# Threshold attention and a gated MLP in one kernel: score matmuls in quadrants with their tail first, and the transposes of q and k as second job

## The chip, the core and the metric

The kernel runs on one core of a Trainium2 chip. The metric is device time in microseconds (us) from one execution of the whole program. Engines are named as in the profile: PE is the matmul engine and PEld its weight loads, DVE the vector engine, ACT the scalar engine, POOL the GpSimd engine, SP the engine whose queue issues most of the DMAs. `L575` means line 575 of the kernel before.

## The reference, cut to what matters

Eight batches, eight heads, 576 rows, head size 64. An attention in which only scores close to their row's maximum survive, then a gated MLP with a mix over the rows:

```
scores = 0.125 * q @ k.T                        # per head, 576 x 576
thresh = max(scores, axis=-1) - tau             # tau = 0.02
scores = where(scores >= thresh, scores, -1e9)
attn   = softmax(scores) @ v
x      = attn with the heads side by side       # 8 x 576 x 512
h      = relu(x @ w_in)                         # 512 -> 1024
u, v   = h[..., :512], h[..., 512:]
v_n    = (v - mean(v)) / sqrt(var(v) + 1e-6)
v_s    = w_spatial @ v_n + b_spatial[:, None]   # 576 x 576 over the rows
out    = (u * v_s) @ w_out                      # float32, 8 x 576 x 512
```

The scores are computed from float32 operands: with a threshold of 0.02 below the maximum, a score decides whether a row of v counts at all. The other products take bf16.

## The kernel before, in words

**Pairs and steps.** Heads are worked on two at a time, 32 pairs `i` in all. Head 0 of a pair lies on partitions 0 to 63, head 1 on 64 to 127. The 576 query rows of a pair are four chunks of 128 rows, `c` = 0 to 3, and 64 rows that remain. The remainders of an even and the next odd pair are put together into one more chunk, `c` = 4. A step is one (i, c): even pairs have the steps 0, 1, 2, 3 and odd pairs 4, 0, 1, 2, 3, which makes 144 steps, numbered from 0 (lines 766 to 768).

**A score** (`scores`, L563). A step writes one tile `s` of three PSUM banks from a pool of two tiles, so the score of step g+2 needs what ACT reads of step g's tile to be finished. For a main chunk there are, for each head, one float32 matmul of 64 x 128 weights against keys 0 to 511 (L575): the two heads take the upper and lower 64 rows of the array. Then the tail, one matmul of 128 x 128 (L578), gives keys 512 to 575 of both heads: its moving operand `kd` is block-diagonal, with the last 64 keys of head 0 in one corner and those of head 1 in the other, copied there by POOL (L269). In a `c` = 4 step there are two pairs, so each matmul has 64 columns of weights and one of two halves of the PSUM partitions. The profile shows a float32 matmul as two passes, so a main score has four rows of L575 and two of L578, and a `c` = 4 score eight and four.

**Behind a score.** DVE takes the negated maximum of each row (L616); ACT makes the exponentials `e` (L639, or L633 and L635 in steps in which ACT also does the threshold); DVE, where ACT has not done it, applies the threshold (L597); a DMA transposes the result into `pT`.

**The jobs of a step.** `step` (L604) first issues the score, then a list `fs` of further jobs. A job is a triple: the engine that takes its result out of PSUM ("act" or "dve"), its matmuls `mm`, and the evacuation `ev`. The first two jobs of the list are issued right behind the score, and those that ACT evacuates have their `ev` there, ahead of the step's exponentials on ACT. Later jobs have their matmuls issued at the end of the step. All results share the pool `ps_f` of two banks (`bank`, L221), handed out in turn: the third job of a step takes the bank of the first one and so waits for its `ev`.

The jobs that matter here:
- `qk_main(i, which)` (L238): four float32 transposes of q or k of the next pair (L246), evacuated by ACT (L251, L253). In steps c = 0 (q) and c = 2 (k).
- `qk_rem(i)` (L256): one transpose with the last 64 rows of q and of k (L261), evacuated by ACT (L264); then POOL makes `kd` (L269). In steps c = 1.
- `pv` (L309) and `pv_rest` (L336): attention times v, 18 bf16 matmuls of 65 or 130 columns (L290, L295), evacuated by DVE (L302, L304).
- `moe_v`, `moe_u`, `moe_s`, `moe_o` (L427 to L557): the MLP of a batch, four or five bf16 matmuls of 512 columns each (L436, L478, L508, L537); the last `u` and `s` are 16 and 20 matmuls of 64 columns (L483, L513), and the last `v` has 64 columns of weights (L421, L424). All are evacuated by ACT but `moe_s`, by DVE.
- `x_pe`, `pr_pe`, `ws_pe` (L360 to L411): bf16 transposes in the first third of the run, evacuated by ACT.

**The order.** The MLP of batch b begins at step 26 + 18 b, one job a step in the order of the string `ORDER` (L781), so the work repeats every 18 steps. The list of a step is put together in lines 838 to 850 with the transposes of the next pair at the head, then the `pv` jobs, then the MLP's. Line 851 sorts it: jobs for ACT ahead of jobs for DVE, `pv_rest` last; the sort keeps the order among equals.

Of the kernel before, what the change touches and what calls it, by code (L numbers as in the profile page):

```python
# [17 lines left out]
def kernel(  # L18
# [17 lines left out]
    nc = tc.nc  # L36
# [6 lines left out]
    P = 128  # L43
# [35 lines left out]
    def clear():  # L79
        nc.vector.memset(kd_ring[0], 0.0)  # L80
        nc.gpsimd.memset(ld_ring[0][2][64:128, :, 4, :], 0.0)
        for t in vx_ring:
            nc.gpsimd.memset(t[0:64], 0.0)
        nc.gpsimd.memset(kd_ring[1], 0.0)
        nc.gpsimd.memset(ld_ring[1][2][64:128, :, 4, :], 0.0)
        for t in v_ring:
            nc.vector.memset(t[:, :, D:D + 1], 1.0)
            nc.vector.memset(t[64:128, 4, D:D + 1], 0.0)
            nc.vector.memset(t[0:64, 5, D:D + 1], 0.0)
            nc.vector.memset(t[64:128, 10, D:D + 1], 0.0)  # L90
        for t in vn_ring:
            nc.vector.memset(t[64:128, 4, :], 1.0)
# [9 lines left out]
    def load(i, n, w, eng=nc.sync):  # L102

        b, hp = divmod(i, HP)
        t = ld_ring[i // 2 % 2][w][:, 2 * (i % 2):2 * (i % 2) + 2 * n]
        src = (q, k, v)[w][b, 2 * hp:2 * hp + 2 * n]

        def main():
            eng.dma_start(
                out=t[:, :, 0:4, :],  # L110
                in_=src[:, 0:512, :].rearrange("h (p c) d -> p h (c d)", c=4))

        def rest():

            u = ld_ring[i // 2 % 2][(0, 0, 2)[w]][(slice(0, 64), slice(64, 128), slice(0, 64))[w]]
            eng.dma_start(out=u[:, 2 * (i % 2):2 * (i % 2) + 2 * n, 4, :],
                          in_=src[:, 512:576, :].rearrange("h p d -> p h d"))

        def rest_b():
            nc.sync.dma_start(  # L120
                out=vx_ring[i // 2 % 2][64:128],
                in_=src.rearrange("(j h) s d -> h s j d", h=2)[1, 512:576])
        return [main, rest] + ([rest_b] if w == 2 else [])

    def view(t, off, dims):

        return bass.AP(t.tensor, t.offset + off, [t.ap[0]] + dims)
# [93 lines left out]
    def bank(dtype=F32, n=512):  # L221
        if wide:

            turn[0] += 1
            if turn[0] % 8 not in (2, 3):
                return wide[0].tile([P, n], dtype, name="t")
        return ps_f.tile([P, n], dtype, name="f")
# [5 lines left out]
    qks, pts, xns, xts = {}, {}, {}, {}  # L233
# [4 lines left out]
    def qk_main(i, which):  # L238
        hold = {}

        def mm():
            if which == 0:
                qks[i] = qkT.tile([P, 2, S], F32, name="qkT")
            t = hold["t"] = bank()
            for c in range(4):
                nc.tensor.transpose(out=t[:, c * P:(c + 1) * P], in_=nat[i][which][:, c, :],  # L246
                                    identity=identf)

        def ev():
            if which == 0:  # L250
                nc.scalar.mul(out=qks[i][:, 0, 0:512], in_=hold["t"], mul=scale)  # L251
            else:
                nc.scalar.copy(out=qks[i][:, 1, 0:512], in_=hold["t"])  # L253
        return "act", mm, ev

    def qk_rem(i):  # L256
        hold = {}

        def mm():
            t = hold["t"] = bank()  # L260
            nc.tensor.transpose(out=t[:, 0:P], in_=nat[i][0][:, 4, :], identity=identf)  # L261

        def ev():
            nc.scalar.copy(out=qks[i][:, :, 512:576],  # L264
                           in_=hold["t"][:, 0:P].rearrange("p (w s) -> p w s", w=2))
            kd = kd_ring[i % 2]
            for lo in (0, 64):
                hs = slice(lo, lo + 64)
                nc.gpsimd.tensor_copy(out=kd[hs, hs], in_=qks[i][hs, 1, 512:576])  # L269
        return "act", mm, ev  # L270
# [292 lines left out]
    def scores(i, c):  # L563

        s = ps_s.tile([P, 1536], F32, name="s")
        if c < 4:
            who = [(i, slice(c * P, (c + 1) * P), slice(0, P))]
        else:  # L570
            who = [(i - 1 + k, slice(512, 576), slice(64 * k, 64 * k + 64)) for k in range(2)]
        for h in range(2):
            hs = slice(64 * h, 64 * h + 64)
            for n, m, rows in who:
                nc.tensor.matmul(out=s[rows, 1024 * h:1024 * h + 512], lhsT=qks[n][hs, 0, m],  # L575
                                 rhs=qks[n][hs, 1, 0:512], start=True, stop=True)
        for n, m, rows in who:
            nc.tensor.matmul(out=view(s[rows], 512, [[448, 2], [1, 64]]), lhsT=qks[n][:, 0, m],  # L578
                             rhs=kd_ring[n % 2], start=True, stop=True)
        return view(s, 0, [[960, 2], [1, S]])  # L580

    def on_act(i, c):
# [21 lines left out]
    def step(i, c, fs):  # L604

        s = scores(i, c)
        while held:
            held.pop(0)()
# [174 lines left out]
    for b in range(B):  # L783
        n = dict.fromkeys("vuso", 0)
        for j, t in enumerate(ORDER):
            f = {"v": moe_v, "u": moe_u, "s": moe_s, "o": moe_o}[t]
# [17 lines left out]
    with tc.manual_schedule():  # L804
        for w in (0, 1):
            for f in load(0, 1, w, (nc.sync, nc.scalar)[w]):
                f()
        make_identity(nc, identf)
        clear()
        nc.vector.memset(ntau, -float(tau))  # L810
        nc.vector.memset(mhalf, -0.5)
        nc.scalar.activation(out=ctau, in_=ntau, func=ACT.Exp)
        nc.vector.tensor_copy(out=identb, in_=identf)
        for w in (0, 1):
            for f in load(1, 1, w):
                f()
        for f in load(0, 2, 2):
            f()
        for j in range(3):
            load_w_in(j)  # L820
        for _ in range(14):
            nc.tensor.transpose(out=ps_f.tile([P, 512], F32, name="f")[:, 0:P], in_=identf,
                                identity=identf)
        shape_first()
        first()
        shape_qk(1)
        queue = []
        for g, (i, c) in enumerate(steps):
            if c == 2 and i + 2 < NPAIR:
                shape_qk(i + 2)  # L830
            if c == 0:
                shape_v(i)
            if c == 0 and i % 2 and i + 3 < NPAIR or g == 0:
                for w in range(3):
                    queue.extend(load(i + (3 if g else 2), 2, w))
            if g in chores:
                chores[g][0](chores[g][1])
            fs, small_ones = [], []
            if i + 1 < NPAIR and c < 3:
                fs.append(qk_rem(i + 1) if c == 1 else qk_main(i + 1, c // 2))  # L840
            if i and c == (2 if i % 2 else 3):
                fs.append(pv(i - 1, 0))
            if i > 1 and c == 4:
                fs.append(pv(i - 2, 1))
            if i % 2 and c == 3:
                fs.append(pv(i - 1, 1))
            if i % 2 and i > 1 and c == 1:
                small_ones = [pv_rest(i // 2 - 1)]
                fs += small_ones
            fs += [f(*a) for f, *a in jobs.get(g, [])]  # L850
            fs.sort(key=lambda f: (f[0] == "dve", f in small_ones))
            sends += queue[:1 if g > 3 else 2]
            del queue[:1 if g > 3 else 2]
            step(i, c, fs)

        def run(*fs):
            for f in fs:
                f[1]()
                f[2]()
                for f in sends:  # L860
                    f()
                sends.clear()
        while held:
            held.pop(0)()
        mask()
        inner.close()
        wide.append(ctx.enter_context(tc.tile_pool(name="ps_t", bufs=6, space=PSUM,
                                                  reuse_waits="tile")))
        for _, f in later:
            f()  # L870
        last = [f(b, j) for f, b, j in last]
        run(last[0], pv_rest(NPAIR // 2 - 1), *last[1:3], x_pe(NPAIR - 2), *last[3:6],
            pv(NPAIR - 1, 0), *last[6:], pv(NPAIR - 1, 1), moe_s(Z - 1, 0), moe_s(Z - 1, 1),
            x_pe(NPAIR - 1, True), *[moe_s(Z - 1, j) for j in range(2, 5)])
        rest = last_gmlp(Z)
        next(rest)
        run(moe_u(Z, 0), moe_u(Z, 1))
        next(rest)
        run(*[moe_u(Z, j) for j in range(2, 5)], *[moe_o(Z - 1, j) for j in range(4)])
        next(rest)  # L880
        next(rest, None)
# [35 lines left out]
```

## Time and profile before

| what | value |
|---|---|
| median of 5 runs | 480.62 us |
| lowest and highest | 479.24 and 485.34 us |
| the profiled execution | 479.62 us |
| its span, first to last instruction | 477.8 us |
| around the span | 1.8 us |
| granted PE clock, mean | 1.00 |
| first and last matmul of a score (L575 and L578) | 8.0 and 434.3 us |
| PE, DVE, ACT busy from 120 to 180 us | 57.75, 53.14, 52.26 us of 60 |
| POOL busy from 120 to 180 us | 30.73 us of 60 |

The profile is of one execution. Its page gives busy times, then the span in 40 slices with the busy share of each in tenths. A timeline has one row per group of instructions that follow each other on an engine: start, length, engine, line, operation, output and inputs, tile of the array (rows * columns), operand shape, count. A wait row names who waited, for whom, the total in us, how often, and the longest. Matmuls are pipelined, so a row's length includes the time until the last result is out; what an operation costs PE is read from the distance between starts.

### The profile page before, as it was taken

To read this page: it belongs to the slowest core of one execution; us is meant where nothing else is said; L and a number is where in the kernel's file an instruction comes from. 1 tells how busy PE (TensorE), PEld (TensorE's weight loads), DVE (VectorE), ACT (ScalarE), POOL (GpSimd) and SP (SyncE) were. 2 spreads that over 40 slices of the span, in tenths; PEclk is the share of its full clock that TensorE was granted. 3 is DMA by queue.
4 is the path that set the end of the run, shared out by engine and by line. 5 is a ranking of instruction groups with operands and counts; after the bars stand their busy time and mean duration, and the time that the engine had idled before them with its cause. 6 is when DMAs were issued, how large, how long until landed. Compare 5 with 4: busy or idle time off the path is not lost.

```text
span 477.8 us, 9901 instructions
## 1 busy us (share of the span) xinstructions
PE 448.0 (94%) x3691; PEld 237.0 (50%) x3691; DVE 409.7 (86%) x563; ACT 390.3 (82%) x677; POOL 226.6 (47%) x403
## 2 busy tenths in 40 slices
PE   7678888889999999999999999999999999999995
PEld 4344545444545545454554545455554545445542
DVE  4989898989889997999889888899889998898573
ACT  4799899999879797888979898788978888797251
POOL 3553344895437543574417652475336743252021
PEclk9999999999999999999999999999999999999999
DMA  7979899969888999888889999987997989677523
GB/s 230 251 167 210 190 234 205 199 149 206 168 194 197 171 208 228 214 164 180 200 165 237 182 215 181 214 174 179 187 214 209 182 182 199 149 113 111 150 88 111
DMA packets 226127, 88.48 MB, mean 185 GB/s; under 512 B 196896, under 2 KB 221600, under 8 KB 226080
## 3 DMA queue, kind: packets, MB, share of 16 engines
q1 hardware_dynamic: 225424, 86.98, 85.7%
q8 instruction: 29, 0.48, 0.4%
q0 software_dynamic: 160, 0.52, 0.3%
q10 hardware_dynamic: 496, 0.36, 0.2%
q14 instruction: 18, 0.15, 0.1%
HBM read 33.31 MB, written 9.44 MB: 89 GB/s over the span
## 4 chain that ended last, share of the span: by engine, by line
PE 49%; DVE 22%; ACT 22%; issue 7%; POOL 0%; POOLq 0%; ACTq 0%; DVEq 0%
PE s L575 16%; DVE negm L616 10%; DVE p L597 7%; PE s L578 6%; ACT e L633 6%; ACT e L639 5%; PE f L295 4%; PE f L478 4%; PE f L246 3%; ACT p L635 2%; PE f L508 2%; PE f L537 2%; PE f L290 2%; ACT vrel L446 2%; ACT pr L635 2%
## 5 line engine op out<-in xcount | busy, mean ns | idle before, releaser
L616 DVE TENSOR_REDUCE negm<-s 128x2 f32<-128x1152 f32 x144 | 194.8, 1353 | 34.8 <-PE s L578 34.4
L575 PE MATMUL s<-qkT 64*128 64x512 f32 (+1 forms) x640 | 161.9, 636 | 14.7 <-ACT e L639 8.2
L597 DVE SCALAR_TENSOR_TENSOR p<-e,ctau 128x1152 bf16<-128x1152 f32 x91 | 132.4, 1455 | 1.2 <-ACT e L639 1.1
L639 ACT ACTIVATE e<-s,negm 128x576 f32<-128x576 f32 x182 | 124.7, 740 | 7.7 <-DVE negm L616 7.1
L578 PEld LDWEIGHTS s<-kd,qkT 128*128 128x128 f32 (+1 forms) x320 | 41.2, 177 | 110.0 <-issue 99.4
L633 ACT ACTIVATE e<-s,negm 128x576 f32<-128x576 f32 x106 | 72.9, 741 | 16.0 <-DVE negm L620 10.6
L269 POOL COPY kd<-qkT 64x64 f32<-64x64 f32 x62 | 27.1, 437 | 101.6 <-ACT qkT L264 99.8
L578 PE MATMUL s<-kd,qkT 128*128 128x128 f32 (+1 forms) x320 | 69.5, 320 | 0.0
L575 PEld LDWEIGHTS s<-qkT 64*128 64x128 f32 (+1 forms) x640 | 41.9, 174 | 46.2 <-ACT e L639 18.0
L454 POOL TENSOR_SCALAR nmean<-sm 128x1 f32<-128x1 f32 (+1 forms) x35 | 16.4, 470 | 65.7 <-ACT vrel L446 65.6
L295 PEld LDWEIGHTS <-pT 128*128 128x128 bf16 x1024 | 41.8, 97 | 8.6 <-issue 5.4
L295 PE MATMUL f<-v,pT 128*128 128x65 bf16 x992 | 44.9, 194 | 0.0
L635 ACT ACTIVATE p<-e 128x1152 bf16<-128x1152 f32 x37 | 43.0, 1163 | 1.2
L137 POOL COPY qn<-ql 128x640 f32<-128x640 f32 x31 | 33.8, 1091 | 14.7 <-DMA ql<-in_k_dram 10.8
L466 POOL TENSOR_SCALAR vn<-vrel,rs,nm 128x512 bf16<-128x512 f32 (+1 forms) x34 | 29.6, 871 | 3.7
L508 PE MATMUL f<-wsT,vn 128*128 128x512 bf16 x125 | 31.0, 379 | 0.0
L290 PE MATMUL f<-v,pT 128*128 128x130 bf16 x124 | 27.2, 219 | 2.9 <-ACT qkT L253 1.4
L478 PE MATMUL f<-xT,w_in 128*128 128x512 bf16 x112 | 28.6, 379 | 0.8 <-DVE xn L304 0.7
L253 ACT COPY qkT<-f 128x512 f32<-128x512 f32 x31 | 18.2, 588 | 12.9 <-PE f L246 12.9
L436 PE MATMUL f<-w_in,xT 128*128 128x512 bf16 x112 | 28.7, 379 | 0.0
L304 DVE TENSOR_TENSOR xn<-f,r 128x256 bf16<-128x256 f32 x62 | 26.3, 425 | 2.1
L157 POOL CAST v<-vl 128x640 bf16<-128x640 f32 x32 | 25.1, 786 | 1.0 <-DMA vl<-in_v_dram 1.0
(168 smaller groups left out, 639.1 us busy)
## 6 DMA issues: line engine op xcount, KB each, us to landing
vl<-in_v_dram SPq DMA_DIRECT2D x16, 512.0 KB, 4.5
ql<-in_q_dram SPq DMA_DIRECT2D x15, 512.0 KB, 4.6
kl<-in_k_dram SPq DMA_DIRECT2D x15, 512.0 KB, 4.7
out_dram<-oo SPq DMA_DIRECT2D x10, 512.0 KB, 4.1
uT<-in_moe_w_in_dram SPq DMA_DIRECT2D x3, 512.0 KB, 6.2
uT<-in_moe_w_spatial_dram SPq DMA_DIRECT2D x2, 576.0 KB, 4.9
vl<-in_v_dram SPq DMA_DIRECT2D x16, 64.0 KB, 4.2
pT<-p SPq DMA_TRANSPOSE x64, 5.4
```

The source lines that it names most:

```text
L137: nc.gpsimd.tensor_copy(out=t, in_=ld_ring[i // 2 % 2][w][:, 2 * (i % 2):2 * (i % 2) + 2].rearrange("p h c d -> p c h d"))
L290: nc.tensor.matmul(out=t[:, at:at + 130], lhsT=pt[:, 4, :], rhs=vt[:, 4:6, :].rearrange("p b d -> p (b d)"), start=True, stop=False)
L295: nc.tensor.matmul(out=t[:, at + 65 * h:at + 65 * h + 65], lhsT=pt[:, 5 * h + j, :], rhs=vt[:, 6 * h + j, :], start=False, stop=(h == 1 an ...
L478: nc.tensor.matmul(out=t, lhsT=w_in[:, m, f * P:(f + 1) * P], rhs=xts[b][:, m, 0:512], start=(m == 0), stop=(m == 3))
L508: nc.tensor.matmul(out=t, lhsT=vn[:, c, f * P:(f + 1) * P], rhs=wsT[:, c, 0:512], start=(c == 0), stop=(c == 4))
L575: nc.tensor.matmul(out=s[rows, 1024 * h:1024 * h + 512], lhsT=qks[n][hs, 0, m], rhs=qks[n][hs, 1, 0:512], start=True, stop=True)
L578: nc.tensor.matmul(out=view(s[rows], 512, [[448, 2], [1, 64]]), lhsT=qks[n][:, 0, m], rhs=kd_ring[n % 2], start=True, stop=True)
L597: nc.vector.scalar_tensor_tensor(out=pt[:, c % 2, :], in0=ef, scalar=ctau, in1=ef, op0=ALU.is_ge, op1=ALU.mult)
L616: nc.vector.tensor_reduce(out=nm, in_=s, axis=AX.X, op=ALU.max, negate=True)
L633: nc.scalar.activation(out=e[:, h, :], in_=s[:, h, :], func=ACT.Prelu, bias=nm[:, h:h + 1], scale=by, alpha=1e30)
L635: nc.scalar.activation(out=pr_ring[i // 2 % 2] if c == 4 else p_ring[2 * (i % 2) + c // 2][:, c % 2], in_=e.rearrange("p h s -> p (h s)"), ...
L639: nc.scalar.activation(out=e[:, h, :], in_=s[:, h, :], func=ACT.Exp, bias=nm[:, h:h + 1])
```

## The change

Two things. First, `scores` issues the tail ahead of the chunks, and each main chunk of 128 query rows is split into two of 64, so that its four matmuls (two heads, two halves) each use a quadrant of 64 rows by 64 columns of the array, as the `c` = 4 score did. The tail keeps its form. In a `c` = 4 step only the order of tail and chunks changes. Second, the sort puts the transposes of q and k behind the other jobs that ACT evacuates, but still ahead of those of DVE. This changes the list of 62 of the 144 steps: in each, the first two jobs are both ACT's, and they change places. The steps in which `qk_main` or `qk_rem` is the only job for ACT keep their list.

```
         s = ps_s.tile([P, 1536], F32, name="s")
+        halves = [slice(64 * k, 64 * k + 64) for k in range(2)]
         if c < 4:
-            who = [(i, slice(c * P, (c + 1) * P), slice(0, P))]
+            who = [(i, slice(c * P + 64 * k, c * P + 64 * k + 64), halves[k]) for k in range(2)]
+            tails = [(i, slice(c * P, (c + 1) * P), slice(0, P))]
         else:
-            who = [(i - 1 + k, slice(512, 576), slice(64 * k, 64 * k + 64)) for k in range(2)]
-        for h in range(2):
-            hs = slice(64 * h, 64 * h + 64)
-            for n, m, rows in who:
-                nc.tensor.matmul(out=s[rows, 1024 * h:1024 * h + 512], lhsT=qks[n][hs, 0, m],
-                                 rhs=qks[n][hs, 1, 0:512], start=True, stop=True)
-        for n, m, rows in who:
+            who = tails = [(i - 1 + k, slice(512, 576), halves[k]) for k in range(2)]
+        for n, m, rows in tails:
             nc.tensor.matmul(out=view(s[rows], 512, [[448, 2], [1, 64]]), lhsT=qks[n][:, 0, m],
                              rhs=kd_ring[n % 2], start=True, stop=True)
+        for h in range(2):
+            for n, m, rows in who:
+                nc.tensor.matmul(out=s[rows, 1024 * h:1024 * h + 512],
+                                 lhsT=qks[n][halves[h], 0, m], rhs=qks[n][halves[h], 1, 0:512],
+                                 start=True, stop=True)
         return view(s, 0, [[960, 2], [1, S]])
...
-            fs, small_ones = [], []
+            fs, small_ones, plain = [], [], []
             if i + 1 < NPAIR and c < 3:
-                fs.append(qk_rem(i + 1) if c == 1 else qk_main(i + 1, c // 2))
+                plain = [qk_rem(i + 1) if c == 1 else qk_main(i + 1, c // 2)]
+                fs += plain
...
-            fs.sort(key=lambda f: (f[0] == "dve", f in small_ones))
+            fs.sort(key=lambda f: (f[0] == "dve", f in small_ones or f in plain))
```

## The prediction

> **What bounds the kernel now.** I read the page first: busy shares, then the 40 slices.
>
> ```profile
> span 477.8 us, 9901 instructions
> PE 448.0 (94%) x3691; PEld 237.0 (50%) x3691; DVE 409.7 (86%) x563; ACT 390.3 (82%) x677; POOL 226.6 (47%) x403
> ...
> PE   7678888889999999999999999999999999999995
> ```
>
> A busy PE is not yet a bound, so the busy times by stretch and the waits come next.
>
> ```profile
> 8.00:60.00 52.00, 42.12 (x328) 22.30 (x329) 44.68 (x54) 44.02 (x66) 22.66 (x40) 1.00 0.91 211
> ...
> 180.00:240.00 60.00, 59.03 (x506) 31.33 (x504) 54.48 (x69) 51.06 (x91) 30.75 (x53) 1.00 0.92 197
> ...
> 300.00:360.00 60.00, 59.27 (x473) 30.59 (x472) 53.31 (x69) 50.76 (x90) 29.12 (x52) 1.00 0.91 189
> ```
>
> ```profile
> DVE negm L616 <- PE s L578: 34.4, 53, 1.7
> ...
> PEld s L575 <- ACT e L639: 18.0, 29, 1.4
> ...
> PE f L290 <- ACT qkT L264: 3.5, 7, 1.4
> ```
>
> The columns after the length of a stretch are PE, PEld, DVE, ACT and POOL. Up to about 75 us (steps 0 to 23) PE has gaps: in the timeline nearly every score begins 0.05 us after the exp that frees its `s` buffer has ended. From step 26 on PE has almost none, and the reduction waits for the score's last matmul (34.4 us). So scores are PE work on the path, but DVE with 53 to 54 us in 60, and ACT with 51, stand close behind: what PE can save before they bind is a few tenths of a us per stretch of steps.
>
> **The score's price.** The timeline around one main score (step 66), columns start and length:
>
> ```profile
> 197.06 0.38 PE L508 MATMUL f<-wsT,vn 128*128 128x512 bf16 x1
> 197.37 1.13 PE L575 MATMUL s<-qkT 64*128 64x512 f32 x4
> 198.43 0.49 PE L578 MATMUL s<-kd,qkT 128*128 128x128 f32 x2
> 198.75 0.38 PE L436 MATMUL f<-w_in,xT 128*128 128x512 bf16 x1
> ```
>
> Starts count, since lengths include the pipeline's end. A 512-column bf16 matmul repeats every 0.216 us (five L508 take 1.24, the last one 0.38 of it), so the score begins 0.09 us after the job's stream: the price of changing the array's form. The chunks hold PE for 1.06, the tail 0.32, and the next job follows with no further gap: 0.09 + 1.06 + 0.32 = 1.48 us.
>
> The four-quadrant form is already in the trace, in the score of two 64-row remainders (c = 4):
>
> ```profile
> 200.81 0.61 PE L575 MATMUL s<-qkT 64*64 64x512 f32 x4
> 201.35 0.44 PE L578 MATMUL s<-kd,qkT 128*64 128x128 f32 x4
> ```
>
> Its first pass started at 200.33, its second at 200.81, the tail at 201.35: 1.02 us with the change of form behind it. Against 1.06 that is only the shorter weight load (64 columns for 128).
>
> **Part 1, tail first and quadrants.** A 128x128 f32 matmul whose load lies behind its predecessor takes 0.11: the four L246 from 205.20 to 205.64. The tail after a form change takes 0.32 because its first load (0.107) is bare. Put behind a job of the same form, the tail costs 0.22, then 0.09 for the change, then 1.02: 1.33, which is 0.148 less. Taken off again are three loads that become bare:
> - 0.08 where the job ahead ends in 64- or 65-column matmuls (they repeat every 0.03 and cannot cover 0.107). The code's order gives 47 of the 105 main scores from step 26 on.
> - The first load behind the quadrants: 0.035 if bf16 (L537 after a c = 4 score loads at 174.07 and starts at 174.11), 83 scores.
> - 0.10 if it is an f32 transpose, 22 scores, and 6 more where the transposes now follow the 64-column matmuls of L421.
>
> PE's stream from step 26 on: 105 x 0.148 - 47 x 0.08 - 83 x 0.035 - 28 x 0.10 = 15.5 - 3.8 - 2.9 - 2.8 = **6.0 us shorter**. The one cost no row shows is whether an f32 load hides behind bf16 matmuls at all; bounds 0 (as behind f32) and 0.107 bare per score. I take hidden, as L578 to L436 and L246 to L246 are. The c = 4 score keeps its three form changes and its matmuls: 0. The tail now waits first for `kd`; POOL copies it two or more steps (over 5 us) ahead: 0, and at most the 1.67 of its longest pair of copies (at 210.18) if POOL falls behind.
>
> The Trainium skill ("TensorE: Matmul & The Clock Gate", Part 3, The mechanism) says that a weight load overlaps running matmuls only if its row group differs. The L246 row disagrees, all 128 rows and still 0.11 apiece. By the rule the tail's load would be bare in every score, 0.107 x 105, and the 6.0 would be gone.
>
> Steps 0 to 23 gain little: when `s` is released, the tail's load is bare, and release to reduction goes from 1.58 (measured) to 0.32 (bare tail) + 0.09 + 0.48 + 0.02 (four starts) + 0.59 (last matmul) + 0.03 = 1.53; about half of the steps are led by this: -0.3 (-1.2 to +0.5, as the jobs behind the score start 0.06 to 0.16 later).
>
> **Part 2, transposes second.** 62 of 144 steps swap two jobs whose results ACT copies. No instruction is added and no DMA is in them; the output DMA of L549 is still put into SP's queue behind the exps. ACT now waits for the longer job first: in step 92 its two idle gaps before the copies (0.16 and 0.28) become one of about 0.66. Steps 90 to 93 are where ACT sets the release of `s` (0.05 to 0.36 us of slack), so PE's 0.38 there is not delivered and about 0.07 per period of 18 steps is lost. POOL's `kd` copies, already waiting 99.8 us for L264, wait some 0.6 longer; behind them stand the casts of q and k for two steps later: 0.
>
> The dear part is the `f` pool, which has two banks. In 15 of the swapped steps a third job takes the bank of the first. Step 96 before (`qk_rem`, `moe_o`, `pv_rest`):
>
> ```profile
> 289.25 1.13 PE L575 MATMUL s<-qkT 64*128 64x512 f32 x4
> 290.31 0.49 PE L578 MATMUL s<-kd,qkT 128*128 128x128 f32 x2
> 290.63 0.27 PE L261 MATMUL f<-identf,qn 128*128 128x128 f32 x1
> 290.74 1.03 PE L537 MATMUL f<-w_o,gT 128*128 128x512 bf16 x4
> 291.27 0.28 ACT L264 COPY qkT<-f 128x128 f32<-128x128 f32 x1
> 291.61 0.22 PE L290 MATMUL f<-v,ptr 128*128 128x130 bf16 x1
> ...
> 291.81 0.58 ACT L546 COPY oo<-f 128x512 f32<-128x512 f32 x1 [0.25 <-PE f L537]
> ...
> 292.31 1.13 PE L575 MATMUL s<-qkT 64*128 64x512 f32 x4
> ```
>
> The short transpose is copied (0.28) while L537 streams, and `pv_rest` starts without a wait, 2.45 us after the job ahead. With `moe_o` first: 1.365 (score and load) + 0.86 (four matmuls) + 0.17 (to the result) + 0.58 (copy) + 0.05 = 3.03; PE is there at 2.34. A wait of 0.69, and `pv_rest` 0.58 later than now, 0.9 if ACT is 0.3 behind by then. Five such steps (60, 78, 96, 114, 132). The step behind each gives about 0.2 back: there `moe_u` (copy 0.38) leads in place of a 0.58 copy, and a wait for DVE's xr goes. Steps 33 and 42 put a 0.71 copy ahead of a 0.28 one: 0.43 each. Steps 25, 34 and 43 trade copies of like length: 0.
>
> **Sum.** Per period of 18 steps PE saves 0.92. Steps 90 to 94 do not deliver 0.38, and some 0.1 is lost in steps 82 to 86, where DVE works without a gap from one reduction to the next: 0.45 x 6.5 periods = -2.9. Bank waits 5 x (0.7 - 0.2) = +2.5 and 2 x 0.43 = +0.9; ACT 6 x 0.07 = +0.4; the first steps -0.3. Together **+0.6 us** on the profiled execution's 479.62, so 480.2. That execution lies 1.0 below the median of five, 480.62; on the median it is **481.2 us**.
>
> **The rivals.**
> - A, faster: the bank waits find cover (ACT has room, DVE was 0.37 late in step 97 anyway) and the 6.0 arrives, with the first steps' 0 to 1.2. Time 480.6 - 6.0 = 474.6, down to 473.4; with half of the 6.0, 477.6. For it: PE's gapless slices. Against: slacks of 0.05 to 0.36 at five of 18 steps.
> - B, slower: the f32 load of the tail is bare in every score. 58 x 0.107 + 47 x 0.03 = 7.6 makes PE's stream 1.6 longer, and nothing is delivered: +0.6 + 2.9 + 1.6 = +5.1, 485.7. For it: the tail's 0.32 today. Against: L246.
> - C, slower: the wait for the first job's bank in the 15 three-job steps. With 0.9 in five, 0.3 in the five behind them, 0.43 in two and 0.3 in three: 4.5 + 1.5 + 0.9 + 0.9 = 7.8, less 2.9 and 0.3, plus 0.4: +5.0, 485.6. It decides from a mean of 0.5 us on (15 x 0.5 = 4.8 + 2.9). For it: the 3.5 us wait of L290 on L264 that is there now. Against: ACT has 51 us in 60.
>
> **How the numbers follow.** Forecast 0.50, A 0.20, B 0.14, C 0.16. About 1% (4.8 us) is what a measurement of this kernel can tell from no change: under 475.8 is faster, over 485.4 slower. Faster: most of A (0.16) and an edge of the forecast (0.03), 0.19. Slower: some 0.6 of B and C (0.18) and an edge of the forecast (0.05), 0.23. Same: 0.58. The range, 475 to 486, leaves out the lower half of A and what of B and C exceeds its price; the forecast alone is 478 to 484.
>
> **What would show it.** Right: main scores of 1.33 to 1.45 us from the tail's start to the next job; the tail's two matmuls 0.11 apart behind 512-column jobs; in steps 60, 78, 96 a gap of 0.6 to 0.9 before L290 put down to ACT's L546; reductions starting later than their score more often. Wrong: tail matmuls 0.21 apart everywhere (B), no gap in step 96 (A), or PE gaps before scores in place of the saved time, then DVE or ACT has taken all of it.

## The result, and the profile after

| | before | after |
|---|---|---|
| median | 480.55 us (95 runs) | 481.31 us (53 runs) |
| lowest and highest | 479.10, 486.02 | 479.29, 485.40 |
| profiled execution | 479.62 us, span 477.8 | 483.99 us, span 482.2 |
| granted PE clock, mean | 1.000 | 0.987 |

The ratio is 1.0018, 95% interval 1.0009 to 1.0028: 0.8 us slower, far inside the 1% that was set as "the same". The forecast was 481.2; how much of that agreement is luck is said further down. The profiled execution of after lies 2.7 us above its median, which has to be kept in mind below.

The page of after (line numbers are now L575 for the tail, L579 for the quadrants, L618 for the reduction):

```profile
span 482.2 us, 10931 instructions
PE 447.4 (93%) x4203; PEld 226.5 (47%) x4203; DVE 411.4 (85%) x563; ACT 387.9 (80%) x677; POOL 223.3 (46%) x403
PE   7788888889899999999999999999997999999995
q8 instruction: 33, 0.54, 0.5%
```

PE has 512 more matmuls, since a main score has eight passes in place of four, and its busy time is the same (though 10.2 us inside the span of after ran at half clock, see the last section). The slices show one new thing: a 7 at slice 31. The last line is the queue that brings instructions; in before it is

```profile
q8 instruction: 29, 0.48, 0.4%
```

so the longer stream costs four more fetches of 16 KB. The 512 added matmuls have 512 weight loads with them, 1024 instructions in four more blocks, so one block holds 256 PE instructions. This line looked like nothing, and it turns out to matter.

The stretches of the same view as before (PE, PEld, DVE, ACT, POOL, then the clock):

```profile
180.00:240.00 60.00, 57.97 (x554) 28.81 (x553) 54.04 (x69) 51.02 (x92) 29.65 (x52) 1.00 0.96 198
300.00:360.00 60.00, 58.57 (x560) 29.51 (x558) 53.18 (x68) 50.90 (x91) 28.84 (x52) 1.00 0.92 189
360.00:420.00 60.00, 56.05 (x521) 28.29 (x518) 50.84 (x65) 47.32 (x85) 26.30 (x49) 0.97 0.87 178
```

PE, 59.0 and 59.3 before in the first two, is now free for 1.4 to 2.0 us of 60, but the other engines get no more done in a stretch: what was saved stands as gaps. The waits say where:

```profile
DVE negm L618 <- PE s L579: 31.2, 52, 1.7
PEld s L575 <- ACT e L641: 16.5, 28, 2.0
...
PEld L290 <- DMA pT<-p: 5.2, 3, 3.4
```

and of PE's own queue:

```profile
PE f L290 <- ACT oo L546: 2.8, 5, 0.6
PE f L290 <- DMA pT<-p: 2.7, 2, 2.5
```

The wait on L546 was foreseen: five times 0.56 us. Those on the transposed `p` were not; before has none.

**Where the time went.** The table adds up the lengths of the steps (from the first score matmul of one step to that of the next, in the timelines) and takes those of before away; us. The kernels of the last columns are described below; half shift is after_ph.

| steps | forecast | after | half shift | keep3 | p1_only | p2_only | unsplit |
|---|---|---|---|---|---|---|---|
| start and 0 to 25 | -0.3 | +0.2 | -0.7 | +0.3 | -0.3 | +0.8 | -0.1 |
| 33, 42 and 34, 35, 43, 44 | +0.9 | +1.0 | +1.4 | -0.2 | -0.4 | +1.3 | +0.1 |
| 60, 78, 96, 114, 132 and the two steps behind each | +2.5 | +0.6 | +0.6 | -1.0 | -1.0 | +1.8 | +1.2 |
| 54, 103, 121 | 0 | +4.7 | +0.9 | +3.0 | +2.0 | +0.8 | +0.5 |
| all others to 142 | -2.5 | -2.1 | -1.9 | -2.0 | +0.4 | +0.2 | -0.5 |
| sum | +0.6 | +4.3 | +0.3 | 0.0 | +0.7 | +5.0 | +1.2 |

The sum of one profile is one execution; the verdicts below go by the medians. The rows also hold 3.4 us stretches in which the granted clock was 0.5, which come in some executions and not in others. One stands in step 34 of after, half shift and p2_only, where the step takes 4.4 to 4.5 us, and 3.3 to 3.4 in all other profiles; and one (in keep3 two in a row) begins in step 4 or 5 of after, keep3 and p2_only.

**Step 82, a score whose tail is hidden** (columns start, length). First before, then after:

```profile
246.30 1.24 PE L508 MATMUL f<-wsT,vn 128*128 128x512 bf16 x5
247.47 1.13 PE L575 MATMUL s<-qkT 64*128 64x512 f32 x4
248.53 0.49 PE L578 MATMUL s<-kd,qkT 128*128 128x128 f32 x2
248.85 0.27 PE L261 MATMUL f<-identf,qn 128*128 128x128 f32 x1
```

```profile
247.43 1.24 PE L508 MATMUL f<-wsT,vn 128*128 128x512 bf16 x5
248.51 0.39 PE L575 MATMUL s<-kd,qkT 128*128 128x128 f32 x2
248.82 1.09 PE L579 MATMUL s<-qkT 64*64 64x512 f32 x8
249.84 1.04 PE L436 MATMUL f<-w_in,xT 128*128 128x512 bf16 x4
```

The five L508 take 1.08 to the score's start, 5 x 0.216: no gap for a change of form (1.17 before). Tail 0.31, quadrants 1.02, and the next job: 1.33, as worked out. The step falls from 2.45 us to 2.32. Behind 65-column matmuls the tail's start to the next job is 1.41 or 1.42, and 1.44 where PE had waited for `s`, even for hundredths of a us, since the load of the tail is then bare too. From the start of the last matmul ahead to the start of the first job behind, a main score that waits for nothing takes 1.55 us for 1.69 behind 512-column matmuls, and 1.45 for 1.51 behind 65-column ones. After the quadrants a bf16 job follows without the 0.035 that I had put down.

**Step 96, the bank wait** (after):

```profile
290.08 0.39 PE L575 MATMUL s<-kd,qkT 128*128 128x128 f32 x2
290.39 1.09 PE L579 MATMUL s<-qkT 64*64 64x512 f32 x8
291.42 1.04 PE L537 MATMUL f<-w_o,gT 128*128 128x512 bf16 x4
...
292.29 0.27 PE L261 MATMUL f<-identf,qn 128*128 128x128 f32 x1
292.49 0.58 ACT L546 COPY oo<-f 128x512 f32<-128x512 f32 x1 [0.23 <-PE f L537]
...
293.13 0.22 PE L290 MATMUL f<-v,ptr 128*128 128x130 bf16 x1 [0.56 <-ACT oo L546]
...
293.74 0.46 PE L575 MATMUL s<-kd,qkT 128*128 128x128 f32 x2
```

L290 starts 3.05 after the score (3.03 forecast). The step is 3.67 us long against 3.07.

**Step 121, the slice with the 7.** Before, the issue of its transposed `p`, the step's start and the use:

```profile
360.31 4.42 SPq L601 DMA_TRANSPOSE pT<-p  x1
...
366.36 1.09 PE L575 MATMUL s<-qkT 64*64 64x512 f32 x8
...
367.75 0.23 PE L290 MATMUL f<-v,pT 128*128 128x130 bf16 x1
```

After:

```profile
361.07 6.39 SPq L603 DMA_TRANSPOSE pT<-p  x1
...
367.10 0.44 PE L575 MATMUL s<-kd,qkT 128*64 128x128 f32 x4
...
367.47 1.09 PE L579 MATMUL s<-qkT 64*64 64x512 f32 x8
...
371.07 0.29 PE L290 MATMUL f<-v,pT 128*128 128x130 bf16 x1 [2.52 <-DMA pT<-p]
```

In before L290 began 1.39 us after the step's start, here 3.98; and behind it the PE clock is lowered for 3.4 us (five L508 take 2.27 for 1.24), so the step has 7.17 us for 3.19. The DMA view of 367.1 to 371.1 (40 slices of 0.1 us):

```profile
DMA  1999999999999999999999999000001000001004
GB/s 38 223 297 289 287 292 289 289 289 287 287 297 287 292 297 289 231 307 207 223 200 200 200 65 13 0 0 0 3 8 10 10 8 10 10 10 18 0 0 41
...
q8 instruction: 1, 0.02, 1.8%
...
pT<-p SPq DMA_TRANSPOSE x1, 10.0
```

All engines carry 256-byte packets of the transpose (290 GB/s) up to 369.5. One instruction fetch stands in the window: by its DMA record it ran from 368.8 to 369.97. After its end a trickle of 10 GB/s goes on to 370.9, less than one of 16 engines gave before (290 / 16 = 18). That reads as packets of the transpose that stood behind the 16 KB on one engine, and PE waits for the last of them. In the packet records the first of them begins at 369.97, where the fetch ends, and 34 follow one another singly, 0.02 to 0.04 us apart, until 370.8.

Two things come together here. The issue of the transpose ends 2.0 us later in relation to the step (6.39 us long for 4.42), and the landing follows 3.56 us after that end, 1.41 in before. The second part is the fetch's: in the fourteen profiles of this case a transposed `p` lands 1.90 us after the end of its issue if no fetch was under way in between (median of 678), and 3.30 us if one was (median of 218); in each profile by itself the two medians are 1.9 and 3.1 to 3.5.

### The profile page after: what moved, and what is told of

Its sections match the earlier page's. It is cut to its first block, busy times and chain, and to the rows that moved or that the text cites. A ratio compares the mean times of both kernels' runs of the same rounds, so it can differ in the third digit from the quotient of the medians.

```text
span 482.2 us, 10931 instructions
## 1 busy us (share of the span) xinstructions
PE 447.4 (93%) x4203; PEld 226.5 (47%) x4203; DVE 411.4 (85%) x563; ACT 387.9 (80%) x677; POOL 223.3 (46%) x403
## 4 chain that ended last, share of the span: by engine, by line
PE 49%; ACT 26%; DVE 14%; issue 5%; DMA 3%; POOL 1%; POOLq 0%; DVEq 0%; ACTq 0%
PE s L579 14%; DVE negm L618 7%; ACT e L635 6%; ACT e L641 6%; PE f L295 5%; DVE p L599 5%; PE s L575 4%; PE f L537 4%; ACT p L637 3%; PE f L246 3%; PE f L478 3%; PE f L508 2%; PE f L436 2%; DMA pT<-p 2%; PE f L290 2%
## 5 line engine op out<-in xcount | busy, mean ns | idle before, releaser
L618 DVE TENSOR_REDUCE negm<-s 128x2 f32<-128x1152 f32 x144 | 194.7, 1353 | 32.5 <-PE s L579 31.2
L579 PE MATMUL s<-qkT 64*64 64x512 f32 x1152 | 158.4, 620 | 0.0
L575 PE MATMUL s<-kd,qkT 128*128 128x128 f32 (+1 forms) x320 | 64.3, 304 | 12.5 <-ACT e L641 6.8
L269 POOL COPY kd<-qkT 64x64 f32<-64x64 f32 x62 | 37.2, 601 | 81.0 <-ACT qkT L264 79.2
L575 PEld LDWEIGHTS s<-kd,qkT 128*128 128x128 f32 (+1 forms) x320 | 42.7, 180 | 27.1 <-ACT e L641 16.5
L454 POOL TENSOR_SCALAR nmean<-sm 128x1 f32<-128x1 f32 (+1 forms) x35 | 11.5, 330 | 93.3 <-ACT vrel L446 90.3
L579 PEld LDWEIGHTS s<-qkT 64*64 64x64 f32 x1152 | 30.0, 131 | 18.3 <-issue 3.0
L137 POOL COPY qn<-ql 128x640 f32<-128x640 f32 x31 | 28.0, 903 | 12.2 <-DVE negm L618 5.9
L446 ACT ACTIVATE vrel<-f 128x512 f32<-128x512 f32 (+1 forms) x34 | 20.1, 591 | 15.7 <-PE f L436 11.9
L508 PE MATMUL f<-wsT,vn 128*128 128x512 bf16 x125 | 32.1, 389 | 0.0
L290 PE MATMUL f<-v,pT 128*128 128x130 bf16 x124 | 27.4, 221 | 4.1 <-DMA pT<-p 2.7
L157 POOL CAST v<-vl 128x640 bf16<-128x640 f32 x32 | 27.5, 858 | 1.4 <-DMA vl<-in_v_dram 1.4
```

The lines of the kernel that those rows point to most:

```text
L508: nc.tensor.matmul(out=t, lhsT=vn[:, c, f * P:(f + 1) * P], rhs=wsT[:, c, 0:512], start=(c == 0), stop=(c == 4))
L618: nc.vector.tensor_reduce(out=nm, in_=s, axis=AX.X, op=ALU.max, negate=True)
```

## The experiments

All were timed in five rounds beside before on the same chip; the ratio is to before, with its 95% interval.

| run | median, us | ratio |
|---|---|---|
| p1_only | 481.34 | 1.0032 (1.0005 to 1.0058) |
| p2_only | 484.01 | 1.0063 (1.0039 to 1.0088) |
| keep3 | 481.56 | 0.9998 (0.9966 to 1.0030) |
| after_again | 482.21 | 1.0033 (1.0007 to 1.0059) |
| keep3_pv | 479.63 | 0.9956 (0.9930 to 0.9981) |
| before_pv | 479.99 | 0.9966 (0.9940 to 0.9993) |
| half_before | 473.28 | 0.9832 (0.9794 to 0.9869) |
| half_after | 475.88 | 0.9886 (0.9850 to 0.9923) |
| after_ph | 479.67 | 0.9978 (0.9962 to 0.9995) |
| unsplit | 482.09 | 1.0038 (1.0018 to 1.0058) |
| combined | 476.60 | 0.9920 (0.9898 to 0.9942) |
| after_ph2 | 482.76 | 1.0047 (1.0032 to 1.0063) |

**p1_only: the scores changed, the sort as before.**

```
-            fs.sort(key=lambda f: (f[0] == "dve", f in small_ones or f in plain))
+            fs.sort(key=lambda f: (f[0] == "dve", f in small_ones))
```

> Part 1 alone: tail first and quadrants, with the job order of before. My theory (PE saves time, DVE and ACT let only a part of it through, and the new job order gives it back in waits for the bank of the first job): PE's stream is still shorter, a little less than in the changed kernel since the transposes' load lies bare behind the quadrants in 75 scores instead of 22, but no bank wait is added. 1 to 2.5 us under the kernel before, ratio 0.995 to 0.998; step 96 back to about 3.0 us. Rival 1 (DVE and ACT take everything, bank waits are of no account): within 0.3 us of the kernel before or of the changed kernel, and no difference between job orders. Rival 2 (the half-clock windows seen in the changed kernel's profile are brought on by the quadrants and cost the time): 1 us or more over the kernel before, with a granted clock under 1.00.

Not faster: 1.0032. The bank waits are gone, step 96 is 2.98. Two things take the gain. Step 121 waits for its transposed `p` here as well (4.70 us). And every other c = 4 step with `pv` and `moe_s` is longer, 49, 85, 103 and 139 by 0.4 and 67 by 0.2, on ACT (step 103):

```profile
310.41 0.44 PE L575 MATMUL s<-kd,qkT 128*64 128x128 f32 x4
...
311.35 0.58 ACT L446 ACTIVATE vrel<-f 128x512 f32<-128x512 f32 x1
311.82 0.19 ACT L446 ACTIVATION_READ_ACCUMULATOR vrel<-f 128x1 f32 x1
...
312.07 0.22 PE L290 MATMUL f<-v,pT 128*128 128x130 bf16 x1 [0.20 <-ACT vrel L446]
```

ACT reads the bank of `moe_v` until 312.01, and PE takes that bank 0.06 later: 1.66 after the step's start for 1.39. With the transposes second (after) `moe_v` of the step ahead ends sooner and ACT's L446 runs 0.55 to 1.22 after the start; L290 is at 1.39 again. So the swap of the jobs, dear in the three-job steps, is needed here. Rival 2 is out: this profile has the quadrants and no lowered clock before its last microseconds.

**p2_only: the sort changed, the scores as before** (the `scores` of before).

> Part 2 alone: the scores of before, the transposes of q and k behind the other jobs of ACT. My theory: the bank waits appear without the gain: 0.6 in steps 60, 78, 96, 114 and 132 of which 0.3 to 0.5 comes back in the two steps behind, 0.4 in 33 and 42: 1 to 2.5 us over the kernel before, ratio 1.002 to 1.005. Rival 1 (bank waits of no account): within 0.3 us of the kernel before, since no instruction is added. Rival 2 (clock, from the quadrants): as the kernel before, clock 1.00.

1.0063, somewhat more than expected, and worse than after: in its profile the swap alone costs 1.8 in the five bank-wait steps with their followers. Of the 1.3 around 33 and 42, 1.1 is step 34, where the clock was lowered from 101.9 to 105.3 us; it was from 20.0 us on, too. These are the scores of before, so the lowered clock does not need the quadrants.

**keep3: transposes second only in steps of two jobs.**

```
+            late = plain if len(fs) < 3 else []
-            fs.sort(key=lambda f: (f[0] == "dve", f in small_ones or f in plain))
+            fs.sort(key=lambda f: (f[0] == "dve", f in small_ones or f in late))
```

> The changed kernel, but in steps of three jobs the transposes stay first (15 steps go back to the order of before, 47 stay swapped). My theory: the waits for the first job's bank go, 0.1 net in five places of steps 60 to 134 and 0.4 in steps 33 and 42: 1 to 1.5 us under the changed kernel, so 480 us, a little under the kernel before (ratio 0.997 to 1.000). Rival 1: equal to the changed kernel (ratio to before 1.001 to 1.003). Rival 2: equal to the changed kernel.

0.9998: within the range, though the interval tells it neither from before nor from after_again, which ran beside it. In step 96 the short copy comes first and `pv_rest` starts 2.38 after the score:

```profile
289.71 0.33 PE L261 MATMUL f<-identf,qn 128*128 128x128 f32 x1
289.88 1.03 PE L537 MATMUL f<-w_o,gT 128*128 128x512 bf16 x3
290.43 0.28 ACT L264 COPY qkT<-f 128x128 f32<-128x128 f32 x1
290.76 0.22 PE L290 MATMUL f<-v,ptr 128*128 128x130 bf16 x1
```

Step 96 is 3.00 (3.67 in after, 3.07 before). Its profile loses all of the steady gain in step 121, 5.55 us.

**after_again: the changed kernel once more.**

> The changed kernel once more, as a control beside the others, and for a second profile. Both my theory and rival 1: ratio to before 1.001 to 1.003, step 96 again 3.67 us, no late DMA in step 121 and at most one window at half clock, since those were accidents of the first profile. Rival 2: again two or three windows of 3.4 us at half clock, and the lost time behind them.

1.0033. The expectation failed where it mattered: step 121 is late again (5.70), and step 103 now too (4.35), so this is not an accident of one execution. The clock was lowered twice, near 25 and 373 us, as rival 2 has it; but p2_only has two such stretches without the quadrants, and p1_only none with them.

**keep3_pv and before_pv: in the c = 4 steps with both, `moe_s` ahead of `pv(i - 2, 1)`.** In keep3_pv:

```
             late = plain if len(fs) < 3 else []
+            if c == 4 and fs and fs[0][0] == fs[-1][0]:
+                late = fs[:1]
```

> The changed kernel with two orders altered: steps of three jobs keep their fp32 transposes first, and in the six c = 4 steps whose jobs are pv(i - 2, 1) and moe_s, moe_s goes first. Theory (with quadrant scores PE reaches pv(i - 2, 1) of a c = 4 step before its transposed p has landed): the transposes get 1.25 us more, the waits of PE for pT fall from 5.5 us to 2 or less, step 121 from 5.55 to 3.2 to 4.3, steps 49, 67, 85, 103 and 139 to about 3.2, and the time is 0.992 to 0.996 of before. Rival one (an instruction fetch or the lowered clock lengthens step 121, the transfer only shows it): step 121 stays above 5 and the time is 0.998 to 1.001. Rival two (the order costs as much at vn or gT as it saves at pT): the steps after 49, 67 and so on get longer by what these get shorter, 0.999 to 1.001.

> The kernel before with only the c = 4 order altered (moe_s ahead of pv(i - 2, 1) where both are in the step). Theory: before has no wait for pT, so nothing is gained: 0.999 to 1.002, steps 49, 67, 85, 103 within 0.15 us of before. Rival (moe_s first is better in itself, whatever the scores): 0.992 to 0.997.

keep3_pv is 0.9956, but its profile shows the wait only shortened: step 121 is 4.82, with PE's wait 1.5 for 2.4 in keep3. And a second late transfer shows, which after has in a smaller form (0.3 us):

```profile
PE f L424 <- POOL w_o L182: 2.3, 1, 2.3
```

In step 54, MLP matmuls of L424 need the last quarter of `w_o`, loaded in step 51 and cast by POOL; it lands 4.6 us after its issue in before, 5.9 in after and 5.8 in half_after. In keep3_pv it lands after 5.4, and POOL's cast then takes 1.76 us for 0.61. PE also comes to the last of these matmuls earlier, 2.1 us into the step for 2.6, since the swap puts them ahead of the transpose; p2_only, with the scores of before, waits 0.26 us there.

before_pv did better than expected, 0.9966, with steps 49, 85, 103, 121 unchanged at 3.19; its profile does not show where that comes from, and this stays open. It lies in the range of the rival (`moe_s` first is better in itself), and keep3_pv is not told from it, so the 0.9956 cannot be put down to the shorter wait.

**half_before and half_after: a lighter reduction.**

```
-        nc.vector.tensor_reduce(out=nm, in_=s, axis=AX.X, op=ALU.max, negate=True)
+        nc.vector.tensor_reduce(out=nm, in_=s[:, :, 0:288], axis=AX.X, op=ALU.max, negate=True)
```

> The kernel before, with the maximum of each row taken over the first 288 keys of each head only (the shift under the exponentials is then another, which changes the output; the number of instructions is the same). VectorE's reduce falls from 1.36 to about 0.75 us in every step. Theory (the steady steps end at the s buffers, by reduce and exponentials, about as often as at PE's own stream): 0.975 to 0.99. Rival (PE's stream alone is the bound): 0.997 to 1.001.

> The changed kernel with the same shortened maximum. Theory (PE's saving of 8 to 10 us goes into waits for the s buffers and for evacuations by VectorE): with VectorE lighter by 0.6 us a step the saving comes through, and this kernel is 4 to 8 us faster than half_before (0.984 to 0.992 of it), with steps 60, 78, 96 and so on no longer than in half_before plus 0.2. Rival one (the saving goes to the late transposed p): the two are within 2 us of each other and step 121 is 5 us or more. Rival two (quadrants save nothing on PE): the two are within 1 us, and PE's busy time is the same in both.

The theory fell. Both are faster than before, mostly in steps 0 to 25 (step 26 begins at 72.3 and 72.7 us for 76.7), but half_after is 2.6 us slower than half_before. Steps 81 to 98 take 54.84 and 54.78 us, 55.24 in before: with DVE freed of 0.6 us a step the steady steps hardly move, and the change still gains nothing there net. Step 78 is 3.67 in half_after, so that wait is ACT's alone. What half_after loses against half_before is step 54 (+2.5, waiting for `w_o`), step 121 (+1.3) and the bank waits with the steps behind them (+1.6). Half_before loses 0.9 in step 103 to a transposed `p` behind a fetch. In the table's row of all other steps half_after is 2.6 us below half_before, where after is 2.1 below before: DVE, which I had named as standing close behind PE, took some 0.5 us of the gain and not the bulk.

**after_ph: the changed kernel, with every later fetch half a block earlier.**

```
+            if 3 <= g < 7:
+                t = ps_f.tile([P, 512], F32, name="f")
+                for _ in range(8):
+                    nc.tensor.matmul(out=t[0:1, 0:1], lhsT=identf[:, 0:1], rhs=identf[:, 0:1],
+                                     start=True, stop=True)
             step(i, c, fs)
```

> The changed kernel with 32 matmuls of one column more, eight ahead of each of steps 3 to 6, where PE waits about 1 us for the s buffer anyway: 128 PE instructions, half of the 256 that one instruction fetch of queue q8 brings, so that every later fetch comes about two steps earlier. Theory (the fetch holds one DMA engine for 1.2 us while the transposed p that PE waits for stands behind it; PE went on 1.05 to 1.3 us after the fetch's end in every run of the quadrant scores): no fetch falls in steps 85, 103, 121 any more, step 121 falls from 5.7 to 7.2 us to 3.2 to 3.7, step 103 stays at 3.2, and the time is 2 to 4 us below that of the changed kernel, 0.994 to 0.999 of before. Rival (the transposed p of step 121 is late in itself, since SyncE issues it slowly or PE is early): step 121 stays at 4.5 or more, PE goes on without a fetch ahead of it, and the time is 1.000 to 1.004.

0.9978 and 479.67 us: work was added, and the kernel is 0.4% faster than after and 0.55% faster than after_again, now below before. Of the 4.1 us between its profile and that of after, 3.8 lie in steps 54, 103 and 121. Fetches fall in steps 79, 83, 99, 105, 118, 123; step 121 is 3.23:

```profile
361.75 4.49 SPq L603 DMA_TRANSPOSE pT<-p  x1
...
368.24 0.23 PE L290 MATMUL f<-v,pT 128*128 128x130 bf16 x1
```

The forecast for step 103 failed: it is 3.85 long and waits 0.7 for `pT` with no fetch near. That transpose was issued 0.8 us later than in after, in 5.10 us for 4.00, and landed 2.19 us after the issue's end. A transpose can be late without a fetch, only by less. In step 121 the issue is shorter than in after as well (4.49 for 6.39), so this run alone does not part the fetch from the issue.

**after_ph2: a whole block earlier, so that the fetches stand where after has them** (64 such matmuls ahead of steps 1 to 6).

> The run with shifted fetches once more, with 64 one-column matmuls instead of 32, ten or eleven ahead of each of steps 1 to 6: 256 PE instructions, one whole fetch, so that every later fetch lies where the changed kernel has it. Theory (the place of the fetch makes the transposed p late): fetches fall in steps 85, 103 and 121 again, steps 103 and 121 together are 1.5 us or more above the 6.4 to 7.1 us that they take without, and the time is back at 1.001 to 1.004 of before. Rival (the added matmuls help by themselves, by what they do to the first steps or to the clock): steps 103 and 121 as in the run with the half shift, and the time is 0.996 to 0.999.

1.0047. Fetches are back in steps 85, 103 and 121, and step 121 is 4.39; PE went on 1.23 us after the fetch's end. Step 103 is 3.23, so the two together are 7.62, 0.5 above after_ph and not the 1.5 that was expected. The medians of the two runs are 3.1 us apart, their profiles 1.6: 0.7 in steps 54, 103 and 121, 2.0 in the first 26 steps (0.7 on the added matmuls in step 0, 1.3 in step 7 at a lowered clock), less 1.1 in steps 33 to 44, where the lowered clock is after_ph's. So the direction is as the theory has it, and the rival's forecast failed, but what the profiles show of the late transfers is less than the medians differ by.

Over all runs: in the seven profiles with a fetch in step 121 (p1_only, after, after_again, keep3, keep3_pv, half_after, after_ph2) that step is 4.39 to 7.17 us and PE goes on 1.09 to 1.23 us after the fetch has ended; in the seven without one (before, p2_only, before_pv, half_before, unsplit, after_ph, combined) it is at most 3.23. The fetch alone is not enough: six of the seven also have one in step 103, and only after_again waits for `pT` there, since in the others the transpose had landed before the fetch began. The plainest pair is keep3_pv and combined, with the same order of jobs and the same issue of step 121's transpose, the first with a fetch, the second without (combined, described below, has 32 added matmuls and an earlier load of `w_o` besides):

```profile
362.06 5.18 SPq L603 DMA_TRANSPOSE pT<-p  x1
...
370.88 0.23 PE L290 MATMUL f<-v,pT 128*128 128x130 bf16 x1 [1.54 <-DMA pT<-p]
```

```profile
359.65 5.21 SPq L603 DMA_TRANSPOSE pT<-p  x1
...
366.75 0.22 PE L290 MATMUL f<-v,pT 128*128 128x130 bf16 x1
```

It lands 3.60 us after the end of its issue in keep3_pv and 1.74 in combined.

**unsplit: tail first, chunks of 64 x 128 as before.** In `scores`, `who = tails`, the 128 rows at once.

> The changed kernel with the main score chunks not split into quadrants: tail first, then the four matmuls of 64 x 128 as before, and the changed order of the jobs. The number of PE instructions is that of before. Theory (what is saved comes from the tail's place, where its load and its change of shape hide, and not from the quadrants): score to first job 1.34 to 1.42 us as in the changed kernel, steps 81 to 98 together within 0.3 us of the changed kernel's 55.14, no fetch in step 121 and that step about 3.2; time 0.996 to 1.001 of before. Rival (the quadrants carry the saving): score to first job 1.45 us or more, the 18 steps 56 us or more, time 1.006 or more.

In between. Step 82 again:

```profile
248.10 0.38 PE L574 MATMUL s<-kd,qkT 128*128 128x128 f32 x2
248.41 1.13 PE L578 MATMUL s<-qkT 64*128 64x512 f32 x4
249.48 1.04 PE L436 MATMUL f<-w_in,xT 128*128 128x512 bf16 x4
```

Tail 0.31 as in after, chunks 1.07 for 1.02: the score is 1.38. So of the 0.13 us that a hidden score gains on before, 0.09 is the tail's place and 0.04 the quadrants. Steps 81 to 98 take 55.49 us (55.14 in after), and the time is 1.0038: a theory that gave the quadrants nothing missed the time. There is no fetch in step 121, and no wait there.

**combined: all of it.** keep3_pv with the half shift, and the last load of `w_o` in step 50:

```
-                   ((36, 41, 46, 51), load_w_o), ((39, 44, 49, 54), shape_w_o)):
+                   ((36, 41, 46, 50), load_w_o), ((39, 44, 49, 54), shape_w_o)):
```

> All that the runs so far point to: the changed kernel, with transposes first in the steps of three jobs, moe_s ahead of pv(i - 2, 1) in the c = 4 steps, the 32 one-column matmuls of the run with shifted fetches, and the last quarter of w_o loaded in step 50 instead of 51. Theory: steps 60, 78, 96 at 3.0, step 54 at 2.9 to 3.1, step 121 at 3.2, no wait of PE for pT over 0.5 us; time 0.987 to 0.992 of before. Rival (what is taken away in one place is waited for in the next): 0.994 or more.

476.60 us, 0.9920: the edge of the expected range, and 4.2 us below before. Steps 54, 103 and 121 are 2.89, 3.23 and 3.23, steps 78 and 96 are 3.00; step 60 is 3.35 and not the expected 3.0. Of the waits for `pT` there remains one of PE's loads, its longest 0.8 and not under 0.5; no matmul waits for `pT`:

```profile
PEld L290 <- DMA pT<-p: 1.0, 2, 0.8
```

Its runs spread from 475.9 to 478.1, those of after from 479.3 to 485.4. How much each of the parts brings beside the others was not separated.

## Why the prediction was right, point by point

The time was right (481.2 against 481.31), but two terms of the sum were wrong by more than the sum itself, with opposite signs: the bank waits (+0.6 for +2.5) and the late transfers (2 us and more, for nothing). The saving of PE's stream was larger than forecast and a smaller share of it arrived. So the mechanism of the scores and of the bank wait was right, and so was ACT's hold on the delivery in step 92; the agreement to 0.1 us is luck.

- **The score's price: right.** 1.33 us where the tail is hidden, measured 1.33; the tail hides behind bf16 matmuls. 0.08 more behind 65-column matmuls: measured 1.41 to 1.42. "The first load behind the quadrants: 0.035 if bf16": measured 0, which I had taken from a c = 4 score. "0.10 if it is an f32 transpose": measured 0.05 (step 81, four L246 take 0.49 to the next job for 0.44). So PE's stream was shortened by more than 6.0: the two terms were 2.9 and 2.8, of which about 1.4 is left, some 10 us. The rows at step 82 give nearly the same: 58 x 0.14 + 47 x 0.06 - 1.4 = 9.5. The Trainium skill ("TensorE: Matmul & The Clock Gate", Part 3, The mechanism) says that a load overlaps only if its row group differs; the tail's load of 128 rows behind L508's 128 rows is hidden in step 82, so here the trace and the rule differ, and the trace decided.
- **Delivery, "0.45 x 6.5 periods = -2.9", with ACT's +0.4: nearly right in sum, at another share.** All other steps gave -2.1 in after (-2.5 forecast), a fifth of the 10 us, where some two fifths of 6.0 were forecast. Where the rest went, in steps 81 to 98: the scores take 0.26 us more from start to next job (bare tails), and the jobs 0.37 less. In steps 84, 86 and 92 PE meets `s` still held by ACT's exps, and the tail's load is bare as well; PE stands 0.9 us ahead of the scores of these 18 steps, 0.5 in before. The remainder was not followed wait by wait.
- **The first steps, -0.3:** -0.3 in p1_only and -0.1 in unsplit, where the clock was not lowered in them; +0.2 in after, where it was.
- **Bank waits, "5 x (0.7 - 0.2) = +2.5": the wait was right, its net was not.** The five steps lost 0.60 each (0.58 forecast), the next step gave back 0.22 (0.2 forecast), and the step behind that 0.27, which I had not looked at: step 98 was 4.04 in before, 3.77 in after. Net +0.6, not +2.5. That the 0.27 was a wait on DVE in before is suggested by half_before, where the step is 3.82; it was not tried further.
- **Steps 33 and 42, +0.9:** the two lost 0.37 and 0.36, and 35, 43 and 44 gave 0.77 back, which I had at 0. After's profile still has +1.0 there, because the clock was lowered in step 34 (0.67 mean from 99.5 to 104.5 us; 1.00 in before from 95 to 104); after_again and after_ph2, without that, have +0.1 and +0.3. The wait itself is one of 1.9 us for ACT's copy `wsT` in step 33, in all seven profiles with that step swapped; in three of them the lowered clock follows it, and in none of the seven others does the clock fall there.
- **Transfers, 0: the term that failed.** No step of the prediction priced what a shorter PE stream does to a DMA that was just in time, nor the instructions that PE gets more of. It named the 512 additional passes only by their starts. after_ph puts a price on the place of the fetches: 0.9978 against 1.0018 (1.0033 in after_again), 2 to 2.7 us; after_ph2 confirms the direction, not the size.

With the fetches moved (after_ph) the change is worth about -1 us, though one transpose is still late there; as it stands it is +0.8.

The rivals: A (bank waits covered) does not hold as such, keep3 and half_after show the wait and its price. B (load bare everywhere) is out, the tail takes 0.31 in step 82. C (a mean of 0.5 and more over 15 steps) is out: the five steps with the steps behind them cost +0.6 in all, 33 and 42 with their followers +0.1 to +0.3 at full clock.

**What stays open.** The fetch accounts for about 1.4 us of a late `pT` (3.30 for 1.90). In step 121 of after, PE is 2.6 us late before the clock is lowered; SyncE's issue of that transpose took 6.39 us (4.42 in before) and ended before the fetch began. Why it takes 4.9 to 6.4 us in these kernels, against 3.9 to 4.6 in most others (5.2 in combined, with no wait), was not tried. That the packets stand behind the fetch on one engine is read from the rate of 10 GB/s, the single packets and the times; the records do not name the engine. Why before_pv is faster than before stays open too.

## What to carry to other kernels

Before a shorter stream on the bounding engine is put down as gain, look for transfers that land just ahead of their use (here `pT`, which in before landed at 366.1 us, 1.6 us ahead of its use in step 121, and `w_o` in step 54): a wait of zero in the profile says nothing of the slack. More and smaller instructions also move the instruction fetches, and a kernel that repeats every so many instructions can lock a fetch onto its tightest transfer; a handful of dummy instructions ahead shows whether that is so. Where jobs share two banks, put the one with the short evacuation first, but look at the two steps that follow before the wait is counted as lost.

## What the runs showed of the hardware

- An f32 weight load of 128 rows hides behind bf16 matmuls of 128 rows and 512 columns (0.31 from tail to quadrants; behind 65-column ones the score takes 0.08 more), and a change of form between bf16 and f32 of the same shape costs nothing (L508 to tail: 5 x 0.216, no gap); between 128 x 128 and 64-row forms the same place cost 0.09.
- A 16 KB instruction fetch takes 0.9 to 2.4 us, and where it falls between the end of a transpose's issue and its landing, the landing comes 3.30 us after that end for 1.90 (medians of 218 and 678). In step 121 PE went on 1.09 to 1.23 us after the fetch's end in all seven profiles that have one there.
- After some of PE's gaps the granted clock is 0.5 for 3.4 us: in after near 19, 101 and 371 us, in p1_only and before not until the last microseconds. Within a profile all these stretches begin on one grid of 3.41 us. Of the twelve that begin before the last microseconds, eleven stand behind a cell of this grid in which PE was busy 0.33 to 0.60 of the time, and one (combined, near 19 us) behind 0.76. Not every such cell is followed by one: keep3 has a wait of 2.4 us in step 121, a cell at 0.50, and no lowered clock. What else decides it was not tried.
